# Biases of the sequence tail added before the exponential, in attention with a mixture of adapters

## The chip, the cores and the metric

One core of a Trainium2 chip runs the whole program. Its engines work side by side, each through its own list of instructions in order: PE (TensorE, matrix products into PSUM), DVE (VectorE), ACT (ScalarE), POOL (GpSimd[...]) and SP (SyncE, which here issues transfers). The metric is the device time of one execution in microseconds (us), the median of several runs; less is better. A profile's span is a little shorter than the time of its run (238.3 us beside 240.13).

## The reference

Eight batches, eight heads, 576 positions, head size 64. Attention with a relative-position bias comes first, then a mixture of eight rank-16 adapters, of which each row uses two.

```python
scores = scale * np.matmul(q, k.transpose(0, 1, 3, 2))        # scale = 1/8
# bucket(|i - j|) : 32 buckets, constant from a distance of 128 on
scores = scores + bias_table[bucket].transpose(2, 0, 1)[None]
attn = softmax(scores)                  # exp(x - max) / (sum + 1e-9)
x = (attn @ v), heads side by side      # (8*576, 512)
# second stage, for each row of x
logits = x @ w_gate                     # 8 experts, the best 2 are kept
w = softmax over the two kept logits
out = x + sum over the two experts e of w[e] * ((x @ A[e]) @ B[e])
```

## The kernel before

A pair is two heads of one batch; there are 32 pairs, four to a batch. The 576 positions are split in 512 ("main") and 64 ("tail"). Scores are kept transposed: keys on partitions, queries along the row. For each pair there are five chunks of 128x1024 scores, each with one exp on ACT: four of 128 main keys against the 512 main queries of both heads, and a fifth (c = 4) whose first half holds the main keys against the tail queries, and whose second half holds the tail keys of both heads against the main queries. Tail keys against tail queries are done once a batch for all pairs (`tt`).

The bias is a product after the exp: exp(s + b) = exp(s) * exp(b). The bias minus that of the last bucket is zero from a distance of 128 on, so only a band of each chunk is multiplied. The tables M, MT, MH and MHT hold exp(b), made at the start by way of DRAM.

```python
def tT_pe(b):                           # tails of k and q, two heads, transposed
    st[(b, "tps")] = ps = msp.tile([128, HP, 2, 64], BF16, name="tps", tag="ms")
    tl = st.pop((b, "tl"))
    for c in range(HP):
        PE.transpose(ps[:, c].rearrange("p w s -> p (w s)"), tl[:, 2*c:2*c+2, :], ident)

def tT_ev(b, e):                        # spread into tiles whose other blocks are zero
    ps, t = st[(b, "tps")], tlTs[b % 2]
    if e < 2:
        s = slice(e * 64, (e + 1) * 64)
        DVE.tensor_copy(t[s, :, 0:2, s], ps[s])
    else:
        DVE.tensor_copy(t[:, :, 2, :].rearrange("p c (w s) -> p c w s", w=2),
                        ps[:, :, 1:2, :].to_broadcast((128, HP, 2, 64)))

def tt_band(b):
    DVE.tensor_tensor(ptt[b], ptt[b], MHT..., op=ALU.mult)

def qk(i, c):
    ...
    else:                               # c == 4
        for g in range(4):
            PE.matmul(sc[:, g*128:(g+1)*128], lhsT=t[:, 0, g*128:(g+1)*128], rhs=tt[:, hp, 1, :], ...)
        PE.matmul(sc[:, 512:1024], lhsT=tt[:, hp, 0, :], rhs=t[:, 1, :], start=True, stop=True)

def softmax_exp(i, c):
    AC.activation(p, st.pop((i, c, "sc")), ACT.Exp, scale=scale)

def band(i, g, part=0):
    if g == 4:
        if part == 0:                   # 128 columns of p
            DVE.tensor_tensor(pt, pt, MT[:, 2*hp:2*hp+2], op=ALU.mult)
        else:                           # 4 x 32 columns of p
            DVE.tensor_tensor(pk, pk, MH[:, hp], op=ALU.mult)
        return
    ...                                 # g < 4: 8 x 64 or 8 x 96 columns times M
```

Each pair goes on with `pv` (50 matmuls of 65 columns, the 65th giving the row sums), `norm1` (reciprocal) and `norm2` (product into x). After the fourth pair of a batch the second stage (`mixture`) runs: x is transposed by PE, evicted by DVE, the gate logits and z = x A are multiplied out, a chain of about a dozen small DVE operations and one exp makes the gate, z is gated, transposed, multiplied by B, and DVE adds x while it evicts (`o_ev`, 128x512), row block by row block, each stored by its own transfer. The tail rows of two batches are done together (`ot`).

Every step is an `add(engine, cost, fn, deps, due, ...)`. A list scheduler in the program itself takes the steps in order of a model time, so costs, latencies and due times decide the order of each engine's list, and nothing else:

```python
def load(i, due, ek="SP", eq="SP"):     # k, q, v of a pair, five buffers each
    a = add(ek, 450, lambda: nat_dma(i, 0, "kf", k, ek), pre[:1], due, 2600)
    ...
load(0, -50, "SP", "ACT"); loadt(0, -49); bias_prep(); weights()
for i in range(NPAIR):
    load(i, t0 - 24 if i > 4 else -22 + i)      # t0 = 5.0 * i
    ...                                 # casts to bf16 on POOL, transposes, 5 chunks, pv, norms
    if hp == 3: mixture(b)              # due = 20.0 * (b + 1) + 9.5
```

Of the kernel before, what the change touches and what calls it, by code (L numbers as in the profile page):

```python
# [27 lines left out]
def kernel(  # L28
# [37 lines left out]
    op = ctx.enter_context(tc.tile_pool(name="outs", bufs=6))  # L66
# [5 lines left out]
    class Op:  # L72
        __slots__ = ("eng", "cost", "lat", "fn", "deps", "due", "ring", "end", "done",
                     "users", "left", "ready", "n")

    LAT = {"PE": 190, "ACT": 190, "DVE": 110, "PL": 200, "SP": 2600}
    ops = []
    rings = {"ms": [2, []], "o": [6, []]}

    def add(eng, cost, fn, deps=(), due=0.0, lat=None, ring=None):  # L80
        o = Op()
        o.eng, o.cost, o.fn, o.due, o.ring = eng, cost, fn, due, ring
        o.lat = LAT[eng] if lat is None else lat
        o.deps = [d for d in deps if d is not None]
        o.end, o.users, o.done, o.ready, o.n = None, [], False, 0.0, len(ops)
        ops.append(o)
        return o
# [16 lines left out]
    tlTs = [cp.tile([128, HP, 3, 128], BF16, name=f"tlT{i}", tag=f"tlT{i}") for i in range(2)]  # L104
    xts = [cp.tile([128, 4, 2, 64], BF16, name=f"xTt{i}", tag=f"xTt{i}") for i in range(2)]
    ident = cp.tile([128, 128], BF16, tag="ident")
# [3 lines left out]
    ge = cp.tile([H, 512], BF16, tag="ge")  # L110
    g_d = nc.dram_tensor("g_d", (H, 512), BF16, kind="Internal")
    gt = g_d.ap()
# [5 lines left out]
    MHr = cp.tile([128, HP, 192], BF16, tag="MHr")  # L118
    A_f = cp.tile([128, 4, E, r], FP32, tag="A_f")
# [18 lines left out]
    def nat_dma(i, h, key, src, eng):  # L138
        b, hp = divmod(i, HP)
        if h == 0:  # L140
            stg[(i, key)] = ldp.tile([128, 4, 2, D], FP32, name=key, tag=key)
        EN[eng].dma_start(out=stg[(i, key)][:, :, h, :],  # L142
                          in_=src[b, 2 * hp + h, 0:S4, :].rearrange("(g p) d -> p g d", p=128))
# [7 lines left out]
    def tail_dma(b, w):  # L151
        if w == 0:
            stg[(b, "tf")] = ldp.tile([128, H, D], FP32, name="tf", tag="tf", bufs=2)
        SY.dma_start(out=stg[(b, "tf")][w * 64:(w + 1) * 64],  # L154
                     in_=(k, q)[w][b, :, S4:, :].rearrange("h p d -> p h d"))
# [7 lines left out]
    def load(i, due, ek="SP", eq="SP"):  # L163
        pre = [g_("ck", i - 5), g_("cq", i - 5), g_("cv", i - 5)]
        a = add(ek, 450, lambda: nat_dma(i, 0, "kf", k, ek), pre[:1], due, 2600)
        R["lk", i] = add(ek, 450, lambda: nat_dma(i, 1, "kf", k, ek), pre[:1] + [a], due, 2600)
        R["lq", i] = add(eq, 450, lambda: q_dma(i, eq), pre[1:2], due + .1, 2600)
        a = add("SP", 450, lambda: nat_dma(i, 0, "vf", v, "SP"), pre[2:], due + 1.0)
        R["lv", i] = add("SP", 450, lambda: nat_dma(i, 1, "vf", v, "SP"), pre[2:] + [a], due + 1.0)

    def loadt(b, due):
        a = add("SP", 600, lambda: tail_dma(b, 0), [g_("ct", b - 2)], due)
        R["lt", b] = add("SP", 600, lambda: tail_dma(b, 1), [g_("ct", b - 2), a], due)
        a = add("SP", 500, lambda: vtail_dma(b, 0), [g_("cvt", b - 2)], due + .5)
        R["lvt", b] = add("SP", 500, lambda: vtail_dma(b, 1), [g_("cvt", b - 2), a], due + .5)
# [13 lines left out]
    def ct_(b, e):  # L189
        st[(b, "tl")] = ntp.tile([128, H, D], BF16, name="tl", tag="tl", bufs=2)  # L190
        bcopy(EN[e], st[(b, "tl")], stg.pop((b, "tf")))
# [8 lines left out]
    def tT_pe(b):  # L200
        st[(b, "tps")] = ps = msp.tile([128, HP, 2, 64], BF16, name="tps", tag="ms")
        tl = st.pop((b, "tl"))
        for c in range(HP):
            PE.transpose(ps[:, c].rearrange("p w s -> p (w s)"),
                         tl[:, 2 * c:2 * c + 2, :], ident)

    def tT_ev(b, e):
        ps, t = st[(b, "tps")], tlTs[b % 2]
        if e < 2:
            s = slice(e * 64, (e + 1) * 64)  # L210
            DVE.tensor_copy(t[s, :, 0:2, s], ps[s])
        else:
            DVE.tensor_copy(t[:, :, 2, :].rearrange("p c (w s) -> p c w s", w=2),
                            ps[:, :, 1:2, :].to_broadcast((128, HP, 2, 64)))
            tlT[b] = t

    def tt_pe(b):
        st[(b, "ttps")] = ps = msp.tile([128, HP, 128], FP32, name="ttps", tag="ms")
        for c in range(HP):
            PE.matmul(ps[:, c, :], lhsT=tlT[b][:, c, 0, :], rhs=tlT[b][:, c, 2, :],  # L220
                      start=(c == 0), stop=True, skip_group_check=True)
# [4 lines left out]

    def tt_band(b):
        DVE.tensor_tensor(ptt[b], ptt[b], MHT.rearrange("p c w s -> p c (w s)"),
                          op=ALU.mult)
# [9 lines left out]
    def T_ev(i):  # L239
        kqT[i] = kqp.tile([128, 2, S4], BF16, name="kqT", tag="kqT")  # L240
        DVE.tensor_copy(kqT[i], st.pop((i, "kqps")))  # L241

    def qk(i, c):
        b, hp = divmod(i, HP)
        t, tt = kqT[i], tlT[b]
# [7 lines left out]
        else:  # L253
            for g in range(4):
                PE.matmul(sc[:, g * 128:(g + 1) * 128],
                          lhsT=t[:, 0, g * 128:(g + 1) * 128], rhs=tt[:, hp, 1, :],
                          start=(g == 0), stop=True, skip_group_check=True)
            PE.matmul(sc[:, 512:1024], lhsT=tt[:, hp, 0, :], rhs=t[:, 1, :],
                      start=True, stop=True)
# [7 lines left out]
    def band(i, g, part=0):  # L267
        b, hp = divmod(i, HP)
        p = probs[(i, g)]
        if g == 4:  # L270
            if part == 0:
                pt = p[:, 384:512].rearrange("p (h q) -> p h q", h=2)
                DVE.tensor_tensor(pt, pt, MT[:, 2 * hp:2 * hp + 2], op=ALU.mult)
            else:
                pk = p[:, 512:1024].rearrange("p (j q) -> p j q", j=4)[:, :, 96:128]
                DVE.tensor_tensor(pk, pk, MH[:, hp], op=ALU.mult)
            return
# [41 lines left out]
    def norm2(i):  # L319
        b, hp = divmod(i, HP)  # L320
        acc, rc = st.pop((i, "acc")), st.pop((i, "rc"))
        if hp == 0:
            xs[b] = xp.tile([128, 5, H, D], BF16, name="x", tag="x", bufs=4)
        DVE.tensor_tensor(  # L324
            xs[b][:, :, 2 * hp:2 * hp + 2, :].rearrange("p s h d -> p h s d"),
            acc[:, :, :, :D], rc.unsqueeze(3).to_broadcast((128, 2, 5, D)), op=ALU.mult)
# [46 lines left out]
    def gate_chain(b, w, nt, pre, due):  # L373
# [3 lines left out]
        def lg():  # L377
            DVE.tensor_copy(sm_(b, w, nt, "lg", [128, nt, E]), S_("lp"))
# [75 lines left out]
    def o_ev(b, t):  # L454
        st[(b, t, "o")] = o = op.tile([128, Dm], FP32, name="o", tag="o")
        DVE.tensor_tensor(o, st.pop((b, t, "dl")), xs[b][:, t].rearrange("p h d -> p (h d)"),  # L456
                          op=ALU.add)

    def o_st(b, t):
        SY.dma_start(out=out[b * S:b * S + S4, :].rearrange("(p j) c -> j p c", j=4)[t],  # L460
                     in_=st.pop((b, t, "o")))
# [13 lines left out]
    def ot_ev(b):  # L475
        st[(b, "ot")] = o = op.tile([128, Dm], FP32, name="o", tag="o")
# [364 lines left out]
```

## Time and profile before

| | |
|---|---|
| time, median of 3 runs | 240.62 us (239.85 to 243.62) |
| span of the profile | 238.3 us |
| moved by transfers | 39.76 MB, 167 GB/s on average |
| exps of 128x1024 on ACT | 160, busy 156.9 us, 1024 ns each |
| band products with M on DVE | 128, busy 67.4 us |
| normalisations (`norm2`) on DVE | 32, busy 26.2 us |
| evictions with x added (`o_ev`) on DVE | 32, busy 21.0 us |

How to read what follows. A page gives the busy time of each engine with its share of the span and its number of instructions, then the span in 40 equal slices with one digit each (9 is 90% busy or more; PEclk is the clock granted to PE, in tenths of full speed). A group line reads: line of the program, engine, operation, out<-in, shape, count, then busy us in all and mean ns of one, then the idle us of the engine just before such instructions and who ended it. A timeline line reads: start us, length us, engine, line, operation, shape, count, and in brackets the idle time before it and its releaser. Lengths of instructions that follow each other can overlap by about 0.1 us, since one starts before the last has quite ended.

### The profile page before, as it was taken

What the parts mean: (1) busy time and instruction counts of PE and PEld (TensorE: products, weight loads), DVE (VectorE), ACT (ScalarE), POOL (GpSimd) and SP (SyncE); (2) the same over time, 40 slices, a digit from 0 to 9 for tenths busy, and PEclk for the clock granted to TensorE, in tenths of its full rate; (3) what the DMA queues carried; (4) which work ended last, traced back from release to release, by engine and by line L of the source; (5) the groups of instructions that cost most, each with busy time, mean ns of one, the idle gap of its engine ahead of it and who ended that gap; (6) DMA issues with size and microseconds to landing.
All of it is one profiled execution on the core that took longest, in us unless ns stands there. A gap on an engine that the chain in (4) does not pass through costs nothing.

```text
span 238.3 us, 7332 instructions
## 1 busy us (share of the span) xinstructions
PE 186.4 (78%) x2841; PEld 127.2 (53%) x2872; DVE 204.6 (86%) x571; ACT 164.8 (69%) x184; POOL 78.2 (33%) x141
## 2 busy tenths in 40 slices
PE   0365599588879887999698878998789879997762
PEld 0233356455555565666575655676557556676520
DVE  3636957689998999999999998999999998998981
ACT  3174558779798778988598868987588879883000
POOL 6352354455060753533614242432343301000000
PEclk9996759999999999999999999999999999999985
DMA  6999999999998898997987936396213000420415
GB/s 145 222 222 262 191 187 198 230 206 230 214 233 205 191 231 256 215 251 217 237 200 227 239 98 163 128 248 168 47 45 135 3 3 0 180 48 3 177 51 169
DMA packets 101083, 39.76 MB, mean 167 GB/s; under 512 B 87088, under 2 KB 96312, under 8 KB 101048
## 3 DMA queue, kind: packets, MB, share of 16 engines
q1 hardware_dynamic: 100776, 39.04, 67.7%
q8 instruction: 22, 0.36, 0.6%
q10 hardware_dynamic: 272, 0.26, 0.4%
q14 instruction: 13, 0.11, 0.1%
HBM read 29.84 MB, written 9.45 MB: 165 GB/s over the span
## 4 chain that ended last, share of the span: by engine, by line
DVE 38%; PE 28%; issue 10%; SPq 8%; DMA 7%; POOL 5%; ACT 1%; another core or an unknown queue 0%; POOLq 0%; DVEq 0%; ACTq 0%
DVE p L281 10%; PE pv L296 8%; DVE x L324 7%; PE sc L250 7%; DMA qf<-in_q_dram 4%; SPq L142 4%; DVE kqT L241 3%; DVE o L456 3%; DVE xT L340 2%; POOL kb L133 2%; SPq L154 2%; PE kqps L237 2%; PE xps L334 2%; PE pv L303 2%; PE dl L452 2%
## 5 line engine op out<-in xcount | busy, mean ns | idle before, releaser
L264 ACT ACTIVATE p<-sc 128x1024 bf16<-128x1024 f32 x160 | 156.9, 1024 | 38.4 <-PE sc L250 29.9
L281 DVE TENSOR_TENSOR p<-p,M 128x512 bf16<-128x512 bf16 (+1 forms) x128 | 67.4, 543 | 4.4 <-ACT p L264 4.2
L296 PE MATMUL pv<-vn,p 128*128 128x65 bf16 x1024 | 51.7, 197 | 12.3 <-DVE x L324 5.9
L296 PEld LDWEIGHTS <-p 128*128 128x128 bf16 x1024 | 41.3, 99 | 28.8 <-issue 7.9
L250 PE MATMUL sc<-kqT 64*128 64x512 bf16 x256 | 52.1, 405 | 3.8 <-DVE kqT L241 1.6
L133 POOL CAST vn<-vf 128x512 bf16<-128x512 f32 x32 | 22.5, 704 | 45.5 <-PE pv L303 32.6
L133 POOL CAST kb<-kf 128x512 bf16<-128x512 f32 x31 | 20.5, 662 | 34.5 <-PE kqps L237 16.2
L237 PE MATMUL kqps<-ident,kb 128*128 128x128 bf16 x128 | 13.3, 230 | 20.1 <-DVE kb L133 9.5
L324 DVE TENSOR_TENSOR x<-pv,rc 128x640 bf16<-128x640 f32 x32 | 26.2, 818 | 0.3
L133 POOL CAST qb<-qf 128x512 bf16<-128x512 f32 x31 | 20.4, 658 | 18.2 <-DMA qf<-in_q_dram 14.3
L241 DVE COPY kqT<-kqps 128x1024 bf16<-128x1024 bf16 x32 | 21.8, 681 | 2.6 <-PE kqps L237 2.1
L456 DVE TENSOR_TENSOR o<-dl,x 128x512 f32<-128x512 f32 x32 | 21.0, 677 | 2.1 <-PE dl L452 1.7
L250 PEld LDWEIGHTS <-kqT 64*128 64x128 bf16 x256 | 12.8, 93 | 18.6 <-issue 8.6
L237 PEld LDWEIGHTS <-kb 128*128 128x128 bf16 x128 | 8.7, 102 | 23.8 <-DVE kb L133 9.5
L452 PE MATMUL dl<-Bb,zT 128*128 128x512 bf16 x32 | 12.1, 393 | 2.5 <-DVE o L456 2.2
L303 PE MATMUL pv<-vn,p 128*128 128x65 bf16 x256 | 14.1, 198 | 0.0
L395 ACT ACTIVATE ex<-df 128x32 f32<-128x32 f32 (+1 forms) x12 | 2.6, 223 | 16.2 <-DVE df L386 16.2
L237 PE MATMUL kqps<-ident,qb 128*128 128x128 bf16 x128 | 13.3, 231 | 0.2
L311 PE MATMUL pv<-vt,p 128*128 128x65 bf16 x256 | 13.3, 194 | 0.1
L334 PE MATMUL xps<-ident,x 128*128 128x128 bf16 x128 | 12.3, 219 | 1.4 <-DVE x L324 0.4
L303 PEld LDWEIGHTS <-p 128*128 128x128 bf16 x256 | 10.8, 100 | 4.7 <-issue 4.5
L427 PE MATMUL zp<-Ab,xT 128*128 128x128 bf16 x128 | 11.2, 220 | 2.7 <-DVE kqT L241 2.1
(83 smaller groups left out, 239.4 us busy)
## 6 DMA issues: line engine op xcount, KB each, us to landing
kf<-in_k_dram SPq DMA_DIRECT2D x64, 128.0 KB, 3.8
vf<-in_v_dram SPq DMA_DIRECT2D x64, 128.0 KB, 3.9
out_dram<-o SPq DMA_DIRECT2D x32, 256.0 KB, 3.2
qf<-in_q_dram SPq DMA_DIRECT2D x31, 256.0 KB, 4.0
tf<-in_k_dram SPq DMA_DIRECT2D x8, 128.0 KB, 4.1
vtf<-in_v_dram SPq DMA_DIRECT2D x16, 64.0 KB, 4.1
tf<-in_q_dram SPq DMA_DIRECT2D x8, 128.0 KB, 4.3
out_dram<-o SPq DMA_DIRECT2D x8, 128.0 KB, 2.4
```

Source lines behind the costliest of these rows:

```text
L133: e.tensor_copy(o, i)
L237: PE.transpose(ps[:, w, j * 128:(j + 1) * 128], t[:, j], ident)
L241: DVE.tensor_copy(kqT[i], st.pop((i, "kqps")))
L250: PE.matmul(sc[:, h * 512:(h + 1) * 512], lhsT=t[s, 0, c * 128:(c + 1) * 128], rhs=t[s, 1, :], start=True, stop=True)
L264: AC.activation(p, st.pop((i, c, "sc")), ACT.Exp, scale=scale)
L281: DVE.tensor_tensor(pm, pm, M[:, 2 * hp:2 * hp + 2, :, x0:x0 + q1 - q0], op=ALU.mult)
L296: PE.matmul(acc[:, h, s, :], lhsT=p[:, o:o + 128], rhs=vn[:, part, h, :], start=(part == 0 and s == 0), stop=False, skip_group_check=True)
L303: PE.matmul(acc[:, h, 4, :], lhsT=p[:, g * 128:(g + 1) * 128], rhs=vn[:, g, h, :], start=False, stop=False, skip_group_check=True)
L324: DVE.tensor_tensor(xs[b][:, :, 2 * hp:2 * hp + 2, :].rearrange("p s h d -> p h s d"), acc[:, :, :, :D], rc.unsqueeze(3).to_broadcast((128 ...
L334: PE.transpose(ps[:, c, t2 * 128:(t2 + 1) * 128], xs[b][:, 2 * half + t2, 2 * c:2 * c + 2, :], ident)
L452: PE.matmul(ps, lhsT=st[(b, "m", "zT")][:, t, :], rhs=Bb, start=True, stop=True)
L456: DVE.tensor_tensor(o, st.pop((b, t, "dl")), xs[b][:, t].rearrange("p h d -> p (h d)"), op=ALU.add)
```

## The change

It means to take the tail's bias products off DVE and to put them on PE, which has more room; and to begin and end the program with less waiting. In six parts:

1. **Log-form biases.** MT, MH and MHT now hold b/scale instead of exp(b). PE adds them to the scores in PSUM with a product by the identity, before the exp, which multiplies by scale. M stays a product after the exp.
2. **Tails.** Tails of k and q are cast (by POOL) into tiles that are already block-diagonal, 128x128 for each pair and each of k and q. They are transposed whole: eight transposes a batch instead of four, and one DVE copy of 128x1024 instead of three smaller ones. Each batch has four tail loads instead of two, half as large.
3. **Last batch.** `final` takes the place of `mixture` for batch 7: x is transposed and evicted pair by pair, main and tail rows share one gate chain, x is added by PE (identity or selection products) for all row blocks but the first, and evictions are shared by DVE and ACT.
4. **Transfers.** The scheduler's model now has one server for all transfers, at most seven in flight, and earliest times ("nb") for each load. Pair 0's q goes to the same queue as k, the bias table is loaded first on ACT's queue, and weights come later. It changes orders only; nothing in the program waits for a time.
5. **Start.** 40 transposes of the identity on PE at the start; the first M rows are spread from SBUF by ACT's queue and the MT rows have a load of their own from DRAM.
6. **Buffers and order.** Output rows are stored two blocks at a time (three double buffers instead of six), x has three buffers instead of four, and the second stage is due 5 model us earlier.

```diff
+    l_d = nc.dram_tensor("l_d", (H, 512), BF16, kind="Internal")
+    MTr = cp.tile([128, H, 64], BF16, tag="MTr")
...
-    def tT_pe(b):
-        for c in range(HP):
-            PE.transpose(ps[:, c].rearrange("p w s -> p (w s)"),
-                         tl[:, 2 * c:2 * c + 2, :], ident)
+    def tT_pe(b, w):
+        for c in range(HP):
+            PE.transpose(st[(b, "tps")][:, w, c, :], tls[b % 2][:, w, c, :], ident)
...
+    def tT_ev(b):
+        tlT[b] = tlTs[b % 2]
+        DVE.tensor_copy(tlT[b], st.pop((b, "tps")))
...
     def tt_pe(b):
+        PE.matmul(ps.rearrange("p c q -> p (c q)"), lhsT=ident,
+                  rhs=MHT.rearrange("p c w s -> p (c w s)"), start=False, stop=True, ...)
-    def tt_band(b):
-        DVE.tensor_tensor(ptt[b], ptt[b], MHT..., op=ALU.mult)
...
     def qk(i, c):
+            PE.matmul(sc[:, 384:512], lhsT=ident,
+                      rhs=MT[:, 2 * hp:2 * hp + 2, :].rearrange("p h q -> p (h q)"), start=False, ...)
-            PE.matmul(sc[:, 512:1024], lhsT=tt[:, hp, 0, :], rhs=t[:, 1, :], start=True, stop=True)
+            PE.matmul(sc[:, 512:1024], lhsT=tt[:, 0, hp, :], rhs=t[:, 1, :], start=True, stop=False, ...)
+            PE.matmul(sc[:, 512:1024].rearrange("p (j q) -> p j q", j=4)[:, :, 96:128],
+                      lhsT=ident, rhs=MH[:, hp], start=False, stop=True, ...)
...
     def band(i, g):
-        if g == 4: (both products)
...
+        e2 = add("DVE", 330, lambda: DVE.tensor_scalar(gl, g_sb, 1.0 / scale, None, op0=ALU.mult), rs, -19)
+        d2 = add("ACT", 480, lambda: AC.dma_start(out=l_d.ap(), in_=gl), [e2], -26, dma=50)
+        m0 = [add("ACT", 400, lambda h=h: mr0(h), [e], -25, dma=300) for h in range(2)]
+        t_ = add("SP", 600, mtr, [d2], -48, dma=800)
...
+            for _ in range(WARM):                      # 40
+                PE.transpose(t, ident, ident)
...
-    def load(i, due, ek="SP", eq="SP"):
+    def load(i):
+        nk = (0, 3000, 7500, 10000, 13000)[i] if i < 5 else 6500 + 1030 * (t0 - 12)
+        nv = (4000, 9500, 12000, 15000)[i] if i < 4 else 6500 + 1030 * (t0 - 8)
...
     def o_st(b, t):
-        SY.dma_start(out=...rearrange("(p j) c -> j p c", j=4)[t], in_=st.pop((b, t, "o")))
+        SY.dma_start(out=...rearrange("(p j) c -> p j c", j=4)[:, t - 1:t + 1], in_=st.pop((b, t // 2, "o")))
...
     def mixture(b):
-        due = 20.0 * (b + 1) + 9.5
+        due = 20.0 * (b + 1) + 4.5
...
-                    [ev, R["tl", b], g_("ex", *pv_), g_("qk", *last)], t0 + c - 1.7 - 100)
+                    [ev, g_("ex", *pv_), g_("qk", *last)] +
+                    ([R["tl", b], R["MT"], R["MH"]] if c == 4 else []), t0 + c - 1.7 - QA)   # QA = 0
...
-        if hp == 3:
+        if hp == 3 and b + 1 < B:
             mixture(b)
+    final(B - 1)
...                                     # in the scheduler
+        if o.dma:
+            dma_free[0] = max(dma_free[0], t + o.cost + 600) + o.dma
+            o.end = dma_free[0] + 1300
```

## The prediction

> **What bounds the kernel now.** I read the page first: engine shares, then the slices.
>
> ```profile
> PE 186.4 (78%) x2841; PEld 127.2 (53%) x2872; DVE 204.6 (86%) x571; ACT 164.8 (69%) x184; POOL 78.2 (33%) x141
> ...
> DVE  3636957689998999999999998999999998998981
> ACT  3174558779798778988598868987588879883000
> ...
> PEclk9996759999999999999999999999999999999985
> DMA  6999999999998898997987936396213000420415
> ```
>
> VectorE (DVE) has the most work, but its digit is 9 only from about 60 us on. So there are three stages: a head, a long middle and a tail after ScalarE (ACT) has gone to 0. The view by stretches of time says what the middle looks like.
>
> ```profile
> 100.00:120.00 20.00, 17.19 (x269) 11.76 (x272) 19.84 (x53) 15.59 (x18) 8.84 (x14) 1.00 0.91 235
> 120.00:140.00 20.00, 17.91 (x288) 12.28 (x290) 19.53 (x55) 17.12 (x21) 7.15 (x12) 1.00 0.71 188
> ...
> 180.00:200.00 20.00, 17.09 (x287) 12.27 (x287) 19.16 (x63) 16.48 (x19) 3.83 (x6) 1.00 0.06 22
> 220.00:238.30 18.30, 9.65 (x96) 5.37 (x96) 12.04 (x39) 0.39 (x2) 0.00 (x0) 0.79 0.38 130
> ```
>
> Columns after the length: busy us of PE, its weight loads, DVE, ACT, POOL, then granted clock, DMA share, GB/s. DVE is busy over 19 of 20 us, also where the DMA share is only 0.06, so DVE and not the transfers bounds the middle. Counting the 160 big exps (five for each of 32 head pairs) by stretches gives 25 of them by 50 us and the last one ending at 216.1 us: 27 pairs in 166 us, 6.15 us a pair. DVE's busy time between 60 and 220 us is 152.7 of 160 us (95.4%), or 5.87 us a pair.
>
> The groups by shape give the price of what the change touches.
>
> ```profile
> L273 DVE TENSOR_TENSOR p<-p,MT 128x128 bf16<-128x128 bf16 x32 | 9.2, 289 | 0.1
> L276 DVE TENSOR_TENSOR p<-p,MH 128x128 bf16<-128x128 bf16 x32 | 8.2, 257 | 0.0
> L211 DVE COPY tlT<-tps 64x512 bf16<-64x512 bf16 x16 | 6.7, 417 | 1.2 <-PE tps L204 0.8
> L228 DVE TENSOR_TENSOR ptt<-ptt,MHT 128x512 bf16<-128x512 bf16 x8 | 3.5, 437 | 0.0
> L213 DVE COPY tlT<-tps 128x512 bf16<-128x512 bf16 x8 | 3.4, 425 | 0.2
> ```
>
> The reader should see that none of these waits (last column near 0): they fill DVE.
>
> Head and tail, from the timeline of ACT:
>
> ```profile
> 12.17 1.02 ACT L264 ACTIVATE p<-sc 128x1024 bf16<-128x1024 f32 x1 [2.36 <-PE sc L250]
> ...
> 17.98 1.02 ACT L264 ACTIVATE p<-sc 128x1024 bf16<-128x1024 f32 x1 [0.76 <-PE sc L258]
> 21.37 1.02 ACT L264 ACTIVATE p<-sc 128x1024 bf16<-128x1024 f32 x1 [2.36 <-PE sc L250]
> ...
> 31.30 1.02 ACT L264 ACTIVATE p<-sc 128x1024 bf16<-128x1024 f32 x1 [2.93 <-PE sc L250]
> ...
> 226.65 0.39 ACT L395 ACTIVATE ex<-df 128x32 f32<-128x32 f32 x2 [10.28 <-DVE df L386]
> ```
>
> Pair 0's first exp starts at 12.2 us, pair 1's at 21.4, pair 2's at 31.3. The chain that ended last goes through two loads of q here, 5.66 us from 23.07 and 5.05 us from 39.55. The DMA share is about 1 all through the head, while k, v and tails of later pairs are issued ahead of that q. After the last exp (216.1) come 22.2 us of DVE work and stores.
>
> **What the Trainium skill says.** (1) "SBUF — State Buffer", section "Who interferes with whom": a DVE instruction with two SBUF inputs contends with a GpSimd instruction that reads SBUF, and one waits for the whole of the other. The trace agrees: the MT product takes 163/216/668 ns (min, median, max), and its mean of 289 lies 73 above the median. It is then not sure that all of the 289 is saved; a POOL cast may hold the next two-input product instead. (2) "TensorE: Matmul & The Clock Gate", section "What's actually happening": the array's clock is halved until it has been busy for about 3.4 us, and again after an idle window. The trace agrees: PE is busy 0.17 us between 18 and 20 us, and the clock is 0.50 from 20 to 26 and again from 30 to 36 us, after the waits for q. (3) "VectorE: DVE Perf Modes", section "Why PSUM operands drop a tier": a copy from PSUM reaches at most the double rate. The kqT copy of 1024 bf16 from PSUM takes 681 ns; the new single tail copy has that shape.
>
> **The change part by part, middle first.** Per pair, DVE loses:
> - MT and MH products: 0.289 + 0.257 = 0.546 us.
> - MHT product, once a batch of four pairs: 0.437/4 = 0.11.
> - Tail evictions: two of 0.417 and one of 0.425 become one of 0.681: (1.259 - 0.681)/4 = 0.145.
>
> Sum 0.80, so 5.87 becomes 5.07 us a pair. The residue of port waits (0.073 + 0.045 by mean less median) may stay: 5.2.
>
> PE gains work. What PE needs now I take from its timeline between 176 and 190 us by start-to-start times: two QK matmuls 0.32, so 1.28 for four chunks; the tail chunk 0.44; eight transposes 0.46; 50 PV matmuls at 8 in 0.26, 1.62; the second stage about 4.7 a batch (20 x transposes, 16 gate, 16 z, 4 zT, 4 output matmuls of 0.31, half of the odd tail's), and tail transposes and products 0.46, together 1.29 a pair. Sum 5.1. The identity matmuls of MT and MH are 128 columns each, like transposes at 0.23/4 = 0.058: 0.12 a pair. Four more tail transposes (0.23) and one of 512 columns (0.31) a batch: 0.135 a pair. Sum 5.35.
>
> ACT needs 5 x 0.925 (from runs of exps, 2 in 1.94 and 1 in 1.02), plus 0.6/4 and a little for the gates: 4.8, unchanged.
>
> So DVE at 5.07 to 5.2, PE at 5.35 and ACT at 4.8 stand close together. The old kernel lost 5% beside a single bound. With three near each other I allow the same over PE's 5.35: 5.6 us a pair. 27 x (6.15 - 5.6) = 14.9 us saved.
>
> **Head.** q of pair 0 is now issued right behind k on one queue, and pair 1's k and q come before any v. The table's load is the first issue on ACT. But MT, MH and MHT now reach the matmuls through their own trip: table lands about 4.6 (3.8 us after an issue near 0.8), 2.1 us of small DVE copies plus a k cast of 0.41 between them to 7.1, the scaling 0.3, a store to DRAM 3.9 (as the store of g_d, 10.15 to 14.08) to 11.4, the load of MTr some 4 to 15.5, the reversing copy 0.3. PE is in order, so pair 0's tail chunk waits for it: its exp near 16.3, and pair 1's first near 17.3, against 21.4. Then pairs 1 to 4 at about 6.5 (colder clock, M copies of 0.54) end at 43.5 instead of 50: 6.5 us saved. The 40 warming transposes run while PE has nothing else.
>
> **Tail.** Batch 7 no longer runs the common second stage. Its x transposes and evictions follow each pair, and two thirds of the chain is shared. From the end of the last exp: PV 0.5, reciprocal 0.2, the two normalisations 0.8, transposes and their ACT evictions 1.5, gate and z matmuls 0.5, the gate chain 2.1 (225.73 to 227.87 before), products, zT and its eviction 2.0, output matmul and three DVE evictions of 0.69 beside two on ACT 2.6, then stores: before, 4.0 us passed from the end of the last eviction (234.3) to the end of the span. Sum 14.2 to 14.7 against 22.2: 7.5 us saved.
>
> Total 14.9 + 6.5 + 7.5 = 28.9; 240.6 - 28.9 = 211.7, called 212.
>
> **The rivals.**
> - DVE stays the bound and PE has more slack than I read. For: a busy PE in this trace is not PE at its peak, and its starts are often late for lack of data. Against: starts of 0.23 for four transposes are steady. It gives 5.07/0.95 = 5.35 a pair, 22 us saved in the middle, about 205.
> - PE takes over fully, with in-order stalls where the tail chunk waits for ACT's two score buffers and for DVE. For: PE is already busy 17 to 18 of 20 us, and the busy sum plus 0.25 a pair is 5.6. Against: it has waits of its own among these. At 5.9 a pair the middle saves 7, about 220.
> - Transfers take the place. For: each tail load is cut in two (four of 64 KB), the queue waits on eight completion counters in turn, and output buffers go from six rows to three double ones, x buffers from four to three. Against: the share sinks to 0.4 and below after 160 us, and bytes hardly change. A few us at most in the middle; in the head it could eat the 6.5: about 218.
> - The MT trip in the head is longer than 11 us (one-partition source of the first M rows, 128-byte rows of MTr): up to 4 us lost, 216.
>
> **Range and chances.** The rivals span 205 to 220. I take 202 to 222 for 8 in 10. The least sure is the pace of the middle: 0.1 us a pair is 2.7 us. For it not to be faster by 2% (under 236), head, middle and tail together would have to save under 5 us, though DVE loses some 20 us of work in a stretch where it is the bound; that needs a wait I have not seen. Faster 0.96, same 0.03, slower 0.01.
>
> **What would show it.** DVE's busy sum down to about 175 to 180 us; middle stretches with DVE near 18.3 of 20 and PE near 18.5; ACT's exps at 5.6 us a pair; no DVE rows for MT, MH and MHT products; the exp of pair 0's tail chunk near 16 us; the time from the last exp to the end near 14.5 us. I am wrong if a middle stretch shows both DVE and PE idle over 15%, if loads end waits of POOL or PE after 60 us, or if the head is no shorter than 50 us for 25 exps.

## The result, and the profile after

The changed kernel takes 231.26 us (median of 4 runs, 230.79 to 231.63) beside 240.50 of the kernel before: a ratio of 0.962, 95% interval 0.959 to 0.965. It is faster, but by 9 us where 29 were predicted, and 231 us lies outside the range of 202 to 222.

The page of the kernel after, engine shares and slices:

```profile
PE 190.7 (83%) x2986; PEld 136.9 (60%) x3019; DVE 186.2 (81%) x480; ACT 166.7 (73%) x189; POOL 87.2 (38%) x151
...
DVE  5136787289997999999989989999989899989461
ACT  3345778397899698889796769988877789885121
...
PEclk9955999799999999999999999999999999999996
DMA  5889997979979978896799795888992012202214
```

DVE lost 18.4 us of work (204.6 to 186.2), but its digit in the middle is still 8 or 9. The stretches of time of the kernel after (busy us of PE, its weight loads, DVE, ACT and POOL, then granted clock, DMA share and GB/s):

```profile
100.00:120.00 20.00, 18.32 (x306) 13.24 (x307) 18.70 (x44) 16.91 (x20) 8.54 (x13) 1.00 0.84 212
120.00:140.00 20.00, 17.58 (x293) 12.71 (x293) 18.67 (x54) 14.81 (x18) 8.38 (x14) 1.00 0.85 212
...
180.00:200.00 20.00, 18.79 (x302) 13.20 (x305) 18.31 (x47) 17.01 (x19) 2.69 (x4) 1.00 0.19 68
210.00:229.30 19.30, 7.99 (x117) 5.23 (x116) 9.29 (x31) 2.86 (x8) 0.00 (x0) 0.90 0.34 122
```

DVE is down from about 19.5 to 18.6 of 20, PE up to about 18.2: both near 93%, neither full.

The stages come from the timeline of ACT, by the ends of the 25th and the 160th big exp (pair 4's last, and the last of all); the middle between them is 27 pairs:

| span of the profile, us | before | after | saved | predicted |
|---|---|---|---|---|
| to the 25th exp | 52.05 | 48.48 | 3.6 | 6.5 |
| 25th to 160th | 164.08 (6.08 a pair) | 161.92 (6.00) | 2.2 | 14.9 |
| from there to the end | 22.19 | 18.92 | 3.3 | 7.5 |
| all | 238.32 | 229.32 | 9.0 | 28.9 |

All three stages missed. The count of the prediction had given 6.15 us a pair for the kernel before; its 25th exp in fact ends at 52.05 and not at 50.

### The profile page after: what moved, and what is told of

It is laid out like the page before. It is cut to its first block, busy times and chain, and to the rows that moved or that the text cites. A ratio compares the mean times of both kernels' runs of the same rounds, so it can differ in the third digit from the quotient of the medians.

```text
span 229.3 us, 7503 instructions
## 1 busy us (share of the span) xinstructions
PE 190.7 (83%) x2986; PEld 136.9 (60%) x3019; DVE 186.2 (81%) x480; ACT 166.7 (73%) x189; POOL 87.2 (38%) x151
## 4 chain that ended last, share of the span: by engine, by line
DVE 47%; PE 27%; DMA 12%; SPq 5%; issue 4%; ACT 1%; POOL 0%; ACTq 0%; POOLq 0%; DVEq 0%
DVE p L295 13%; DVE x L338 8%; PE pv L310 7%; PE sc L266 6%; DVE o L473 6%; DMA kf<-in_k_dram 4%; DVE kqT L255 4%; PE kqps L249 4%; DMA tf<-in_q_dram 3%; DVE xT L355 3%; DMA Mr<-ge 2%; DVE rc L330 2%; SPq L582 2%; DVE mk L414 2%; PE xps L349 2%
## 5 line engine op out<-in xcount | busy, mean ns | idle before, releaser
L286 ACT ACTIVATE p<-sc 128x1024 bf16<-128x1024 f32 x160 | 156.7, 1023 | 38.6 <-PE sc L266 19.1
L295 DVE TENSOR_TENSOR p<-p,M 128x512 bf16<-128x512 bf16 (+1 forms) x128 | 69.0, 555 | 3.1 <-ACT p L286 2.6
L310 PEld LDWEIGHTS <-p 128*128 128x128 bf16 x1024 | 41.3, 99 | 23.1 <-issue 12.5
L266 PE MATMUL sc<-kqT 64*128 64x512 bf16 x256 | 50.8, 395 | 3.9 <-ACT p L286 2.8
L255 DVE COPY kqT<-kqps 128x1024 bf16<-128x1024 bf16 x31 | 21.2, 683 | 10.5 <-PE kqps L249 10.4
L338 DVE TENSOR_TENSOR x<-pv,rc 128x640 bf16<-128x640 f32 (+2 forms) x33 | 26.4, 802 | 0.8
L141 POOL CAST qb<-qf 128x512 bf16<-128x512 f32 x31 | 21.6, 696 | 6.8 <-DMA qf<-in_q_dram 4.1
L473 DVE TENSOR_TENSOR o<-dl,x 128x512 f32<-128x512 f32 x28 | 18.5, 674 | 1.1 <-PE dl L468 0.9
L141 POOL CAST tl<-tf 64x512 bf16<-64x512 f32 x16 | 10.9, 680 | 12.5 <-DMA tf<-in_q_dram 12.0
L271 PE MATMUL sc<-tlT,kqT 128*128 128x128 bf16 x128 | 12.5, 221 | 0.9 <-ACT p L286 0.8
L317 PEld LDWEIGHTS <-p 128*128 128x128 bf16 x256 | 11.0, 98 | 3.0 <-issue 1.6
L325 PEld LDWEIGHTS <-p 128*128 128x128 bf16 x256 | 10.8, 98 | 3.0 <-issue 1.1
L279 PE MATMUL sc<-MH,ident 128*128 128x128 bf16 x32 | 7.1, 220 | 4.9 <-DVE MH L574 3.5
```

Of the source, the lines that this page charges most:

```text
L141: e.tensor_copy(o, i)
L255: DVE.tensor_copy(kqT[i], st[(i, "kqps")])
L266: PE.matmul(sc[:, h * 512:(h + 1) * 512], lhsT=t[s, 0, c * 128:(c + 1) * 128], rhs=t[s, 1, :], start=True, stop=True)
L271: PE.matmul(sc[:, g * 128:(g + 1) * 128], lhsT=t[:, 0, g * 128:(g + 1) * 128], rhs=tt[:, 1, hp, :], start=(g == 0), stop=True, skip_group_ ...
L295: DVE.tensor_tensor(pm, pm, M[:, 2 * hp:2 * hp + 2, :, x0:x0 + q1 - q0], op=ALU.mult)
L310: PE.matmul(acc[:, h, s, :], lhsT=p[:, o:o + 128], rhs=vn[:, part, h, :], start=(part == 0 and s == 0), stop=False, skip_group_check=True)
```

## The experiments

Each starts from the kernel after unless said otherwise. Ratios are to the kernel before on the same chip; on the chips of the experiments it took 241.2 to 241.7 us in place of 240.5, so bare differences of times understate a gain by about 1 us. "Pace" is us a pair between the 25th and 160th exp; DVE and PE are their busy us a pair in that stretch; "tail" is from the last exp to the end. Times are medians of all runs and ratios use the fast ones alone, which matters for e3 (median of its two fast runs 224.5) and e6 (229.2); the profile of e14 fell in a slow run and is not read.

| run | time | ratio, 95% interval | 25th | pace | DVE | PE | tail |
|---|---|---|---|---|---|---|---|
| before | 240.5 | | 52.05 | 6.08 | 5.81 | 5.30 | 22.2 |
| after | 231.26 | 0.962 [0.959, 0.965] | 48.48 | 6.00 | 5.59 | 5.57 | 18.9 |
| e1 no identity products | 227.10 | 0.948 [0.938, 0.959] | 46.95 | 5.91 | 5.54 | 5.49 | 19.0 |
| e2 doubled | 232.13 | 0.967 [0.959, 0.974] | 49.07 | 5.98 | 5.52 | 5.71 | 19.1 |
| e3 a fourth fewer M products | 226.18 | 0.935 [0.922, 0.947] | 47.18 | 5.78 | 5.20 | 5.55 | 18.8 |
| e4 short v casts | 229.37 | 0.952 [0.941, 0.964] | 48.30 | 5.92 | 5.49 | 5.57 | 19.3 |
| e9 short k, q, v casts | 224.72 | 0.929 [0.923, 0.935] | 48.83 | 5.75 | 5.26 | 5.59 | 19.2 |
| e5 log form undone | 234.04 | 0.969 [0.962, 0.976] | 47.33 | 6.12 | 5.93 | 5.54 | 19.1 |
| e6 other costs for the order | 229.92 | 0.951 [0.946, 0.957] | 49.38 | 5.86 | 5.37 | 5.57 | 19.2 |
| e7 head and tail mended | 223.03 | 0.924 [0.919, 0.929] | 44.52 | 5.92 | 5.54 | 5.61 | 17.7 |
| e8 last stage undone | 230.23 | 0.956 [0.949, 0.962] | 48.57 | 5.94 | 5.54 | 5.59 | 18.5 |
| e15 = e8, later due | 229.57 | 0.954 [0.949, 0.959] | 48.31 | 5.83 | 5.37 | 5.47 | 21.8 |
| e10 = e7 + e6 | 225.87 | 0.935 [0.928, 0.942] | 44.12 | 5.93 | 5.49 | 5.60 | 17.8 |
| e11 = e10, scores first | 225.98 | 0.939 [0.931, 0.947] | 43.56 | 5.96 | 5.48 | 5.56 | 19.6 |
| e12 = e7, fourth chunk in log form | 230.72 | 0.954 [0.946, 0.961] | 44.63 | 6.22 | 5.37 | 5.85 | 17.0 |
| e13 = e12, order of e6 | 225.44 | 0.933 [0.926, 0.941] | 45.54 | 5.91 | 5.21 | 5.76 | 17.8 |
| e14 = before, earlier due | 242.19 | 1.003 [1.000, 1.005] | | | | | |

The intervals of e2, e4, e5, e8 and e12 overlap that of the kernel after, 0.959 to 0.965, so what sets these five apart from it in time is not clear of noise. A pace comes from one profiled execution. In the traces of before, after, e1 to e4 and e15 most records of one matmul of 512 columns a pair are missing (after has 2986 matmuls beside 3019 weight loads, e9 3019 of both), and PE's busy time there is about 0.05 us a pair too low: the matmuls of the tail chunk fill 0.50 us a pair in after and 0.55 in e8.

### Which engine sets the pace: e1, e2, e3, e4, e9

e1 keeps the identity products of the first pair and batch only, so the tail biases are missing from the rest. e2 adds each table twice, at half its size (the result is the same).

```diff
-            PE.matmul(sc[:, 384:512], lhsT=ident, rhs=MT[...], ...)
+            if i == 0: PE.matmul(...)                     # e1; MH and MHT alike
+            for _ in range(2): PE.matmul(...)             # e2, with gl = 0.5 / scale
```

> Leaves out the identity products that add the tail biases (MT and MH from pair 1 on, MHT from batch 1 on), so those biases are missing; every other instruction and all orders stay. PE loses about 0.12 us a pair and 0.25 us a batch, some 5.5 us of its work in all. Theory 'DVE is still the bound' (D): same as the changed kernel within 1.5 us, 230 to 231.5. Theory 'PE took over' (P): 4 to 7 us shorter, 224 to 227.

> The identity products are each done twice with tables of half the size (the same sums). PE gains the same 5.5 us of work, DVE and all orders stay. Theory D: within 1.5 us of the changed kernel, 230 to 232.5. Theory P: 4 to 7 us longer, 235 to 238.

e3 leaves out the M product of the fourth main chunk from pair 4 on. e4 casts only 2 of the 64 columns of v for each head from pair 4 on, e9 the same for k, q and v: the number of casts stays, and the attention is then computed from stale data.

```diff
     def band(i, g):
+        if g == 3 and i >= 4: return                      # e3
-        bcopy(EN[e], vnb[i][:, :, :, 0:D], stg.pop((i, "vf")))
+        w = D if i < 4 else 2                             # e4; e9 also for k and q
+        bcopy(EN[e], vnb[i][:, :, :, 0:w], stg.pop((i, "vf"))[:, :, :, 0:w])
```

> Leaves out the band product of the fourth chunk from pair 4 on (its bias is missing): 28 DVE products of 128x512, 0.495 us long each, 0.41 us start to start, so 11.5 us of DVE's time; PE, ACT and POOL do the same. Theory D: 8 to 11 us shorter, 220 to 223. Theory P: at most 3 us shorter, 228 or more. Theory L (no engine, but the chain from exp to band product to PV to normalisation in order): 3 to 6 us shorter.

> From pair 4 on POOL casts only 2 of 64 columns of v (the rest of v stays that of four pairs before, so the output is another): about 0.6 us less POOL work a pair, nothing else changed. If waits at the SBUF port that DVE and POOL share hold a good part of DVE's time, the mean of the 512-wide band product falls from 495 to 460 ns or less and the time by 3 to 6 us, 225 to 228. If not, the time is the same within 1.5 us and the product keeps its length.

> From pair 4 on POOL casts only 2 of 64 columns of k, q and v (the rest is that of earlier pairs, so the output is another); orders and all else stay. About 1.8 us less POOL work a pair. Upper limit of what the port shared by DVE and POOL costs. If that is what eats the middle, band products fall to about 420 (512 wide) and 560 ns (768 wide) from 495 and 615, and the time by 6 us or more, to 225 or less. The shorter v cast alone gave about 2 us; by that measure 4 to 5 us, 226 to 228.

Measured: without the identity products PE's busy sum is 3.8 us less (186.9) and the time 4.2; with them doubled it is 7.0 more (197.7) and the time only 0.9, both sums by the page. One product less for each pair on DVE gives 5.1 (6.8 by the median of 224.5); POOL's work in the middle cut to half, though POOL is busy only 38% of the span, gives 6.5. Relief of PE, of DVE and of POOL each gains something, so no one engine is the bound. Why as much work added to PE cost so little stays open. The stretches of e9 show what comes next:

```profile
100.00:120.00 20.00, 19.68 (x328) 14.09 (x326) 18.07 (x47) 18.18 (x21) 4.41 (x14) 1.00 0.88 233
...
140.00:160.00 20.00, 19.67 (x313) 13.58 (x311) 18.72 (x47) 18.23 (x21) 3.84 (x14) 1.00 0.85 227
```

With less in DVE's way, PE (first busy column) reaches 19.7 of 20: at a pace of 5.75, PE's 5.59 us a pair are next. In the kernel after, DVE and PE end each other's waits. Two of these waits between 60 and 200 us (waiter, releaser, us in all, times, longest):

```profile
PE pv L310 <- DVE x L338: 3.8, 8, 1.1
...
DVE rc L330 <- PE pv L325: 2.5, 3, 1.3
```

In this stretch no wait of DVE or ACT is ended by POOL, and of PE only 0.7 us of its weight loads. So what e9 gains most likely goes by the length of DVE's own instructions.

The groups by shape between 60 and 200 us show what POOL does to DVE. The kernel before, the kernel after, and e9:

```profile
L281 DVE TENSOR_TENSOR p<-p,M 128x512 bf16<-128x512 bf16 x45 | 20.0, 444 | 0.3 <-ACT p L264 0.2
```

```profile
L295 DVE TENSOR_TENSOR p<-p,M 128x512 bf16<-128x512 bf16 x48 | 23.3, 486 | 0.2
```

```profile
L298 DVE TENSOR_TENSOR p<-p,M 128x512 bf16<-128x512 bf16 x49 | 20.4, 416 | 0.4
```

The same product takes on average 42 ns more after the change, and 70 less than that with POOL's casts shortened. The median is 415 or 416 in all three: it is single products that take much longer. "SBUF — State Buffer", section "Who interferes with whom", of the Trainium skill says that a two-input DVE instruction and a POOL instruction that reads SBUF exclude each other; here are sizes for it. The change itself added to POOL's work: busy 78.2 to 87.2 us, mostly because 7 casts of tails of 128x512 (4.4 us) became 16 of 64x512 (10.9 us). That this is why the product grew is not shown: e6 and e7 have the same casts, and there its mean is 455 and 452, against 444 before the change and 486 after.

### Log form alone: e5

```diff
-            PE.matmul(..., lhsT=ident, rhs=MT / MH / MHT ...)
+            DVE.tensor_tensor(pt, pt, MT..., op=ALU.mult)       # after the exp, as before
```

> Undoes part 1 alone: MT, MH and MHT hold exp(b) again and are DVE products after the exp, PE adds nothing; tails, last batch, transfers and start stay as changed. The recorded prediction prices the log form at 0.66 us of DVE a pair, 17 us and more. Theory S (a short product costs DVE its start-to-start time, 0.133 us, not its length of 0.257 to 0.289): DVE gains only 0.35 us a pair, so 3 to 8 us longer in the middle, and the head some 2 to 3 us shorter because pair 0's tail chunk no longer waits for tables; in all 231 to 236. The recorded sizes: 242 or more.

The log form is worth 2.8 us by the times and 1.5 by the ratios, which is not clear of noise. The pace differs by 0.12 us a pair, and the head by 1.1 us the other way, since there PE waits for the tables. In e5's profile the granted clock is 0.83 between 130 and 140 us, where that of the kernel after is 1.00, so part of the 0.12 is not the log form's. DVE's busy time differs by 0.33 us a pair, half of the 0.66 that the prediction put to these three products. The reading is that a length in the profile is not what an instruction costs. The timeline of DVE of the kernel before:

```profile
195.08 0.21 DVE L273 TENSOR_TENSOR p<-p,MT 128x128 bf16<-128x128 bf16 x1
195.21 0.22 DVE L276 TENSOR_TENSOR p<-p,MH 128x128 bf16<-128x128 bf16 x1
195.35 0.42 DVE L281 TENSOR_TENSOR p<-p,M 128x512 bf16<-128x512 bf16 x1
```

Lengths of 0.21 and 0.22, starts 0.13 and 0.14 apart. Over 60 to 200 us the median from start to start is 0.133 for MT and 0.135 for MH, 0.334 for MHT. "VectorE: DVE Perf Modes", section "The DRAIN you can't avoid", of the Trainium skill says that the next operation does not start until the pipeline is empty, and that one "that is not held starts earlier"; here it starts some 80 ns before the record of the one in front ends. The medians leave out the waits: counted each from its start to the next start, or to its own end if that comes first, the three products fill 0.49 us a pair of the middle before the change, and 0.45 in e5. Of that 0.45 only 0.33 is gained, because DVE's other work fills 0.12 more in the kernel after; why is open.

### Order: e6, e10, e11

e6 changes only model costs in the scheduler: scores 325 instead of 400 (550 for 560), products of M 100 more, the reciprocal 130 instead of 70, PE by 0.42 ns a column. e10 is e6 with e7's mends; e11 is e10 with all scores due 100 model us earlier.

```diff
-            a = add("PE", 400 if c < 4 else 560, lambda: qk(i, c), ...)
+            a = add("PE", 325 if c < 4 else 550, lambda: qk(i, c), ...)
-        a = add("DVE", 70, lambda: norm1(i), prev, t0 + 8)
+        a = add("DVE", 130, lambda: norm1(i), prev, t0 + 8)
```

> The same instructions; only the scheduler's costs are nearer to measured start-to-start times (transposes 56 ns instead of 69, the score chunks 325 and 550 instead of 400 and 560, gate matmuls 26 instead of 33, 100 ns more for each band product, 130 instead of 70 for the reciprocal), so the orders of the engines' lists differ. Theory O (no engine is full; pace is set by lists in an order made for too slow a PE): 3 to 8 us shorter, 223 to 228. Theory D (DVE's work itself): within 2 us of the changed kernel.

> The two mends of e7 and the order of e6 together, computing all of the reference. If the gains add up: head and tail 8 us, middle 3 us more, 219 to 222. If the middle's pace is DVE's work alone, no better than e7 (223).

> As e10, with the score matmuls first in PE's list whenever they are ready (as before the change, where their due time was 100 earlier). If ACT's waits for scores (some 1 us a pair of 6) lie on the chain, 2 to 4 us shorter than e10; if DVE's order is what counts, the same or longer.

The order alone moved the pace by 0.13 us. One thing in it can be named: where reciprocal and normalisation stand one behind the other. Timeline of DVE of the kernel before, then after:

```profile
142.29 0.21 DVE L316 RECIPROCAL rc<-pv 128x10 f32<-128x10 f32 x1
142.43 0.49 DVE L281 TENSOR_TENSOR p<-p,M 128x768 bf16<-128x768 bf16 x1
```

```profile
151.22 0.22 DVE L330 RECIPROCAL rc<-pv 128x10 f32<-128x10 f32 x1
151.47 0.82 DVE L338 TENSOR_TENSOR x<-pv,rc 128x640 bf16<-128x640 f32 x1
```

Before, another product stands between and starts 0.14 us behind the reciprocal; after, the product that needs it starts 0.25 behind. The medians are 0.130 and 0.245, and 0.131 in e6. But e10, with e6's order and e7's mends, has a pace of 5.93, no better than e7's 5.92, and a time of 225.9 beside 223.0: the gains of order and mends do not add up. Differences of 0.1 us a pair between orders are of the size of what was looked for, and e11 gave nothing.

### The head, and the stores of the end: e7

After the change pair 0's tail chunk was exponentiated at 19.9 us, not near 16.3. Timeline of ACT of the kernel after:

```profile
7.95 1.02 ACT L286 ACTIVATE p<-sc 128x1024 bf16<-128x1024 f32 x1 [1.10 <-PE sc L266]
12.88 0.48 ACTq L547 DMA_DIRECT2D Mr<-ge  x1
13.41 1.02 ACT L286 ACTIVATE p<-sc 128x1024 bf16<-128x1024 f32 x1 [4.44 <-DMA vf<-in_v_dram]
...
19.89 1.02 ACT L286 ACTIVATE p<-sc 128x1024 bf16<-128x1024 f32 x1 [3.62 <-PE sc L279]
```

and of DVE, then PE:

```profile
14.87 0.44 DVE L572 COPY MT<-MTr 128x512 bf16<-128x512 bf16 x1 [2.06 <-DMA MTr<-l_d]
18.55 0.56 DVE L568 COPY M<-Mr 128x768 bf16<-128x768 bf16 x1 [3.24 <-DMA Mr<-ge]
19.11 0.43 DVE L574 COPY MH<-MHr 128x512 bf16<-128x512 bf16 x1
```

```profile
19.59 0.27 PE L279 MATMUL sc<-MH,ident 128*128 128x128 bf16 x1 [3.50 <-DVE MH L574]
```

Read from the end: PE waited 3.5 us for MH. MH's copy stood in DVE's list behind that of M, which waited for the second transfer of M rows out of SBUF. ACT, which issues it, stood from 8.97 to 12.88 before that issue, with its next exp behind it; what that issue waited for is not certain from the trace (the first transfer of M rows landed near 12.3). MT itself was there at 15.3, as predicted. At the end of the program, two evictions waited 2.1 us each for one of three store buffers. e7 mends both: M's first rows go through DRAM on the queue of the other loads, and five buffers.

```diff
-        m0 = [add("ACT", 400, lambda h=h: mr0(h), [e], -25, dma=300) for h in range(2)]
+        m0 = [add("SP", 400, lambda: mr(0, 2), [d], -49, dma=600)]      # store of ge due first
-        m1 = add("SP", 400, lambda: mr(2, H), [d], -18, dma=1800)
+        m1 = add("SP", 400, lambda: mr(2, H), [d], -18, nb=14000.0, dma=1800)
-        o = op.tile([128, Dm], FP32, name="ol", tag="ol", bufs=3)
+        o = op.tile([128, Dm], FP32, name="ol", tag="ol", bufs=5)
```

> Two small mends: five buffers instead of three for the last batch's output rows, and the first M rows come from DRAM by the SP queue (as before the change), not from one partition of SBUF by ACT's queue. In the changed kernel the last two evictions waited 2.15 us for a store, and pair 0's tail chunk waited until 19.6 us for DVE, which stood behind the second load of M rows (18.5 us). Expected: tail 2 us shorter (17 instead of 18.9 us after the last exp), pair 0's tail exp 2 to 4 us earlier; in all 3 to 6 us, 225 to 228. If the head is set by loads of k and q further on, only the 2 us of the tail.

Timeline of ACT of e7:

```profile
7.94 2.86 ACT L286 ACTIVATE p<-sc 128x1024 bf16<-128x1024 f32 x3 [0.99 <-PE sc L266]
12.38 1.02 ACT L286 ACTIVATE p<-sc 128x1024 bf16<-128x1024 f32 x1 [1.58 <-PE sc L266]
14.86 1.02 ACT L286 ACTIVATE p<-sc 128x1024 bf16<-128x1024 f32 x1 [1.46 <-PE sc L279]
```

The first three exps run in one go, the tail chunk's starts at 14.9, and the 25th exp ends 4.0 us sooner. The time is 223.03, 8.2 us less than after. Of the 7.2 us between the spans, 4.0 are the head, 1.2 the end, and 2.0 a pace of 5.92 for 6.00, which the mends don't explain and which is within what an order makes. This version computes everything and is the best found.

### The last stage: e8, e15, e14

e8 gives the last batch the common second stage again, with everything else of the change. (The last pair's earlier due time and its normalisation in two parts, which belong to the new stage, go with it.)

```diff
-        if hp == 3 and b + 1 < B:
+        if hp == 3:
             mixture(b)
-    final(B - 1)
```

> Undoes part 3: batch 7 gets the common second stage again. The recorded prediction gives part 3 7.5 us of the tail; the two profiles show 3.3 (22.2 against 18.9 us after the last exp). Expected 3 to 4 us longer, 234 to 236; if the old tail was long for other reasons (a DVE with a backlog), 231 to 233.

The new last stage is worth nothing that shows: the tail is 18.5 us without it and 18.9 with it. The tail's gain must then come from another part. e15 also sets the due time of the second stage back to + 9.5; e14 is the kernel before with + 4.5.

```diff
-        due = 20.0 * (b + 1) + 4.5
+        due = 20.0 * (b + 1) + 9.5
```

> As e8 (the common second stage for the last batch as well), but the second stage is due at 20 x (batch + 1) + 9.5 again, as in the kernel before, instead of + 4.5. It changes orders only and computes everything. Theory A, the earlier due gave what the tail gained: with 9.5 the evictions of batch 6 stand again among the last pair's work, the last reciprocal comes 5 to 6 us after the last exp (e8: 2.9; before: 5.5), and the time from the last exp to the end is 21 to 22.5 us (e8: 18.5; before: 22.2). Theory B, the tail is shorter for another reason (three double output buffers, stores two rows at a time): it stays at 18 to 19.5 us and the last reciprocal comes within 4 us. Time by A 232 to 235 us, by B 229 to 232.

> The kernel before with one number changed: the second stage is due at 4.5 instead of 9.5 model us after its batch. If the tail's gain came from there, the time from the last exp to the end falls from 22.2 to about 19 us and the whole by 2 to 4 us, 237 to 239. If it came from part 3, 240.5 as before.

Timeline of DVE of e15 behind the last exp, which ends at 205.65:

```profile
208.42 1.89 DVE L473 TENSOR_TENSOR o<-dl,x 128x512 f32<-128x512 f32 x3 [0.48 <-PE dl L468]
210.22 0.21 DVE L330 RECIPROCAL rc<-pv 128x10 f32<-128x10 f32 x1
210.35 0.63 DVE L473 TENSOR_TENSOR o<-dl,x 128x512 f32<-128x512 f32 x1
210.89 0.82 DVE L338 TENSOR_TENSOR x<-pv,rc 128x640 bf16<-128x640 f32 x1
```

Batch 6's output evictions stand among the last pair's work again, its reciprocal comes 4.6 us after the last exp (2.9 in e8), and the tail is 21.8 us: the earlier due time is what shortened the tail. But the time is 229.57, no more than e8's 230.23, because the pace is 5.83 for 5.94: 27 pairs give back 3.0 us. The due time moves the second stage's work from the tail into the middle, for nothing in all: 28 of the `o` evictions (128x512) lie between the 25th and the 160th exp in e8 and 24 in e15, and DVE's busy time there is 5.54 and 5.37 us a pair. Nor did e14 gain: 242.19, ratio 1.003.

### One more product to PE: e12, e13

If moving products from DVE to PE pays, the fourth main chunk's is the next: its band is 64 columns of each block of 128, so a table ML in log form and two identity products of 256 columns replace the product, from pair 8 on. e13 is the same with e6's costs.

```diff
+            if c == 3 and i >= 8:
+                for h in range(2):
+                    PE.matmul(sc[:, h*512:(h+1)*512]...[:, :, 64:128], lhsT=ident, rhs=ML[:, 2*hp+h], start=False, ...)
...
-            if c < 4:
+            if c == 3 and i >= 8: R["bd", i, 3] = x       # no product on DVE
+            elif c < 4:
```

> On e7: the band of the fourth chunk gets the log form too, from pair 8 on (PE adds 2 x 256 columns by the identity, no DVE product; one more table load of 512 KB). Computes all of the reference. DVE loses 0.41 to 0.49 us a pair, PE gains 0.22. By e3 (11.5 us of DVE's time less gave 5) and e2 (5.5 us of PE's time more cost 1): 2 to 4 us shorter than e7 (223.0), 219 to 221. If PE's work counts as much as DVE's: the same as e7 or longer.

> e12 in the order of e6's costs. e6's order gained 1 us on the changed kernel and lost 3 on e7 (e10); here DVE has more room: within 2 us of e12 either way.

No gain: DVE fell to 5.37 and 5.21 us a pair, PE rose to 5.85 and 5.76, and the times are 230.7 and 225.4 beside e7's 223.0 (e10, which has e13's order, took 225.9). Most of e12's loss is the trip of the new table; the waits of e12 between 14 and 60 us:

```profile
ACT p L294 <- PE sc L268: 12.1, 10, 4.2
...
DVE ML L579 <- DMA MLr<-l_d: 3.6, 1, 3.6
PE kqps L251 <- DVE xTt L374: 3.6, 1, 3.6
```

(waiter, releaser, us in all, times, longest). DVE stood 3.6 us for ML, PE behind it, ACT behind PE. From the 25th to the 40th exp e12 takes 23.1 us and e7 16.7. Past that, to the 160th, e12 takes 144.9 and e7 143.3: a PE at 5.85 gives nothing for a DVE at 5.37.

## Why the prediction was wrong

**The step that failed** is the first of the change part by part: "Sum 0.80, so 5.87 becomes 5.07 us a pair". DVE's busy time in the middle fell by 0.21 us a pair, from 5.81 to 5.59. To see where the rest went, each DVE instruction of the middle is counted from its start to the next start, or to its own end if that comes first. The parts then add up to the busy sums:

| DVE, us a pair in the middle | before | after |
|---|---|---|
| products of MT, MH and MHT | 0.49 | 0 |
| tail evictions | 0.24 | 0.13 |
| products of M | 1.84 | 1.92 |
| reciprocals of `norm1` | 0.14 | 0.19 |
| second stage | 1.82 | 2.04 |
| `norm2` and evictions of k and q | 1.26 | 1.31 |

- *Work priced by its length.* What was taken away filled 0.60 (0.49 and 0.11), not 0.80: DVE's records overlap, and the sum took lengths for DVE where it took start-to-start times for PE. By e5 the three products are worth even less, 0.33 for the 0.66 of the sum.
- *Work that the sum left out.* The second stage fills 0.22 more of the middle. Its due time, 5 model us earlier, was part of the change and had no price. Between e8 and e15 only that due time differs, and the second stage fills 1.99 and 1.81: 0.18 of the 0.22. The remaining 0.05 are batch 7's evictions of x, which the new last stage does pair by pair.
- *The residue of port waits, 0.073 + 0.045.* The prediction let it "stay", at 5.2. In fact the products of M grew by 0.08. The 512-wide one did so without the log form too (495 ns in e5), so this is not the waits of MT and MH coming back. e9 ties the length of these products to POOL's casts; why it grew from before to after is open.
- *An order that the sum left out.* The reciprocal stands directly before the product that needs it: 0.05 a pair.
- With 0.04 more for `norm2` and the evictions of k and q, 0.60 - 0.22 - 0.08 - 0.05 - 0.04 gives the 0.21.

So a part of what the middle failed to gain is the same work that shortened the tail. With the due time of before (e15) the middle takes 157.3 us, 6.7 less than before the change, and the tail 21.8, only 0.4 less.

**PE** gained 0.27 us a pair of busy time (predicted 0.25; in e8's trace the identity products and the four more transposes a batch fill 0.23), but from 5.30 by its busy sum, and not from the 5.1 that I had from start-to-start times. The allowance of 5% over 5.57 to 5.59 gives 5.87, not 5.6. Measured was 6.00, 7% above both DVE and PE. The rival "PE takes over, 5.9 a pair" came nearest the pace, but its mechanism is not what e2 shows (7.0 us more work for PE: 0.9 us of time). What the runs showed in place of one bound is two engines at 93% that end each other's waits; e9 and e3 relieved DVE and came to 5.75 and 5.78, 3 to 4% above PE's busy time.

**Head.** MT's trip of 15.5 us was right (copied at 15.3), and so was the risk named in the last rival, the one-partition source of the first M rows: pair 0's tail chunk came 5.0 us later than in e7 (19.9 for 14.9). What was missed is where it strikes: M's late transfer holds up MH, since the copies stand in one list, and ACT's exps, since ACT issues it.

**Tail.** The sum had PV at 0.5 us after the last exp. The last reciprocal comes 3.9 us after it, since the last pair's PV starts 1.3 us after it, when the normalisation of the pair in front is done, and then takes 2.6 us with other matmuls between. Timeline of DVE after:

```profile
214.28 0.22 DVE L330 RECIPROCAL rc<-pv 128x10 f32<-128x10 f32 x1 [1.15 <-PE pv L325]
...
224.84 0.69 DVE L141 COPY ol<-pv 128x512 f32<-128x512 f32 x1 [2.15 <-DMA out_dram<-ol]
```

From the reciprocal to the end it is 15.0 us (13.7 to 14.2 predicted), with the wait for a store buffer of 2.15 in it; e8, with the old stage, needs 15.65. So of the 7.5 us put to the new stage 0.6 are gained there, and 1.0 lost ahead of it, where e8's last reciprocal comes 2.9 us after the last exp. What the tail did gain is the due time's (3.3 us between e8 and e15), and e15 shows it taken from the middle.

**Right:** that it is faster, PE's added work, the end of DVE's rows for MT, MH and MHT, and that loads do not bound the middle: no wait of PE, DVE or ACT between 60 and 200 us is ended by one. The sign named against this, loads that end waits of POOL after 60 us, did show (11.0 us by loads of k alone), but POOL has room: PE, DVE and ACT waited next to nothing for it.

**Open:** why orders that differ little give paces from 5.83 to 6.00, and so how much of e7's 223.0 is order. No run moves POOL's casts elsewhere; e9 puts their cost to DVE at 6.5 us at most, as it also leaves POOL less work.

## What to carry to other kernels

Price an instruction that is to be removed by the time from its start to the next start, not by its length: for the three products here the lengths promised twice what e5 shows. Price a due time too: when it moves work from one stage into another, the one stage gains what the other loses. When the removed work brings two engines level, expect a pace above both (7% here). And before an issue is given to an engine that computes, look at what it has to wait for, and at what stands behind it in that list.

## What the runs showed of the hardware

- A small two-input product on DVE (128x128 bf16) takes 0.133 us from start to start (median) and 0.21 or more by its record; a product that needs the reciprocal just in front of it starts 0.245 behind that reciprocal's start, an independent one 0.13.
- The first M rows, 96 KB out of a single partition into 128, took about 5.4 us (issued 6.87, landed near 12.3), and ACT, asked for a second such issue, did no exp for 4.4 us.
- Cutting POOL's casts from 2.4 to 1.2 us a pair shortened the 512-wide DVE product from 486 to 416 ns on average and the run by 6.5 us, at a POOL share of 38%.
